# Keeping the emitted order on every engine, and emitting the softmax three superblocks ahead, late in the pass

## The chip, the cores and the metric

The kernel runs on one core of one Trainium2 chip. The time is device time in microseconds (us) of that core; a kernel's time is the median of its timed runs. The profile and trace are of one execution; its span (first to last instruction) lies about 2 us below the time.

Engines: PE is TensorE (PEld its weight loads), DVE is VectorE, ACT is ScalarE, POOL is GpSimd, SP is SyncE, which issues the loads and stores of this kernel (SPq in the profile).

## The reference

A dynamic convolution over time, then a feed-forward block. Cut to what matters:

```python
w = exp(weight_gen - max);  w = w / sum(w)              # softmax over K = 7 taps, per head
x_pad = zeros for K-1 steps, then x                     # each batch starts with zeros
y[b, s, h, g] = sum_k w[b, s, h, k] * x_pad[b, s + k, h, g]
h = y @ w_in                                            # 192 -> 2048
out = (h - tanh(h)) @ w_out                             # 2048 -> 192
```

There are 8 batches of 4096 steps and 32,768 tokens. The kernel works in 32 superblocks of 1024 tokens, 4 to a batch.

## The kernel before

Six stages work on different superblocks at once: load, softmax (exp on ScalarE; sum, reciprocal, multiply on VectorE, giving `wsm`), products (GpSimd, seven of them, giving `prod`), transposes with the sum over taps (`conv`: TensorE into PSUM, ScalarE copies to `convT`), first matmul with h - tanh(h) (`gemm1`: TensorE `ph`, ScalarE `th`, VectorE `gt`), second matmul (`gemm2`: TensorE `po`, ScalarE `out_sb`, store). Where `manual_schedule` doesn't hold an engine, a scheduler in the build may reorder that engine's instructions.

```python
    # every pool below has bufs=2: wgpool (wg_t, e_t, zsum, zr, wsm), xpool, ppool (prod0..6), opool (out_sb)
    # psum_h bufs=3 (ph and pc share it), psum_o bufs=2

    def load(n):                       # wg_t: 128 partitions
        ...
        lo = 0
        if s == 0:                     # first superblock of a batch: partition 0 has no history
            lo = 1
            nc.vector.memzero(x_t[0:1, 0:HALO, :])
            nc.sync.dma_start(out=x_t[0:1, HALO : HALO + J, :], in_=x[b, 0:J]...)
        ...
        nc.sync.dma_start(out=x_t[lo:P, :, :], in_=src)     # 127 partitions if s == 0

    def softmax(n):
        nc.scalar.activation(out=e_t, in_=wg_t, func=ACT.Exp)
        nc.vector.reduce_sum(out=zsum, in_=e_t)
        nc.vector.reciprocal(zr, zsum)
        nc.vector.tensor_mul(wsm, e_t, zr)

    def products(n):                   # 7 instructions on GpSimd
        for k in range(K):
            nc.gpsimd.tensor_mul(prod[k], x_t[:, k : k + J, :], wsm[:, :, :, k : k + 1])
    ...
    order = tc.manual_schedule(engines={mybir.EngineType.PE})
    ctx.enter_context(order)           # TensorE keeps the emitted order, the scheduler orders the rest
    ...
    for n in range(NTOT + 1):          # "pass n"
        if n + 2 < NTOT:
            softmax(n + 2)
            products(n + 2)
        if n + 3 < NTOT:
            load(n + 3)
        for p in range(J):             # J = 8
            gemm1(n, 2 * p); gemm1(n, 2 * p + 1)
            gemm2((n - 1) * J + p)
            if p == 2: conv(n + 1, (0, 1))
            if p == 5: conv(n + 1, (2,))
```

The softmax here doesn't subtract the row's maximum and nothing guards it: scores larger than these inputs give would overflow.

## Time and profile before

| | before |
|---|---|
| time, median | 1441.03 us (1439.78 to 1442.24) |
| span of the profiled run | 1437.9 us |
| busiest engine | TensorE, 58% |
| ordinary superblock | 40.9 us |
| four superblocks (a batch) | 174.1 us |

The page's first part gives busy time, share of the span and number of instructions of each engine; the groups give source line, engine, operation, shapes and count, then busy time and mean duration in ns, then the engine's idle time just before them and what ended most of it:

```profile
PE 837.2 (58%) x16640; PEld 639.2 (44%) x16640; DVE 662.3 (46%) x616; ACT 643.0 (45%) x865; POOL 654.4 (46%) x247
...
L124 POOL TENSOR_TENSOR prod<-x_t,wsm 128x1536 bf16<-128x1536 f32 x224 | 643.1, 2908 | 685.1 <-PE pc L147 613.3
L110 DVE TENSOR_TENSOR wsm<-e_t,zr 128x448 f32<-128x448 f32 x32 | 25.3, 792 | 352.1 <-POOL prod L124 352.1
```

No engine is near its limit. GpSimd is idle for 685 us, of which 613 end with TensorE's transposes; VectorE is idle for 352 us in front of 32 small multiplies, 23 times until GpSimd's products end. Each waits for the other.

### The profile page before, as it was taken

To read this page: it belongs to the slowest core of one execution; us is meant where nothing else is said; L and a number is where in the kernel's file an instruction comes from. 1 tells how busy PE (TensorE), PEld (TensorE's weight loads), DVE (VectorE), ACT (ScalarE), POOL (GpSimd) and SP (SyncE) were. 2 spreads that over 40 slices of the span, in tenths; PEclk is the share of its full clock that TensorE was granted. 3 is DMA by queue.
4 is the path that set the end of the run, shared out by engine and by line. 5 is a ranking of instruction groups with operands and counts; after the bars stand their busy time and mean duration, and the time that the engine had idled before them with its cause. 6 is when DMAs were issued, how large, how long until landed. Compare 5 with 4: busy or idle time off the path is not lost.

```text
span 1437.9 us, 36105 instructions
## 1 busy us (share of the span) xinstructions
PE 837.2 (58%) x16640; PEld 639.2 (44%) x16640; DVE 662.3 (46%) x616; ACT 643.0 (45%) x865; POOL 654.4 (46%) x247
## 2 busy tenths in 40 slices
PE   0033526774556755556755556655557753568997
PEld 0012425553444544444544445544345542456776
DVE  0034524553444544444544444544435553447783
ACT  0022424552444544444544444544335543456884
POOL 3098455433555315555145553445544435544700
PEclk9996868886888878888788888888878887788999
DMA  4321211112110121101211020110301102012011
GB/s 68 88 69 50 75 38 43 68 49 87 67 40 31 54 82 69 68 5 55 79 68 68 9 94 35 69 69 13 115 9 69 68 17 103 20 45 85 25 46 46
DMA packets 16951, 81.18 MB, mean 56 GB/s; under 512 B 4128, under 2 KB 8224, under 8 KB 12712
## 3 DMA queue, kind: packets, MB, share of 16 engines
q1 hardware_dynamic: 13712, 76.51, 14.1%
q0 software_dynamic: 3088, 2.36, 1.3%
q8 instruction: 130, 2.13, 0.6%
q14 instruction: 21, 0.17, 0.0%
HBM read 56.06 MB, written 25.17 MB: 56 GB/s over the span
## 4 chain that ended last, share of the span: by engine, by line
PE 38%; POOL 30%; DMA 14%; DVE 6%; another core or an unknown queue 5%; issue 5%; ACT 1%; POOLq 0%; DVEq 0%; ACTq 0%
POOL prod L124 30%; PE po L200 18%; PE ph L170 15%; DMA out_dram<-out_sb 12%; PE pc L147 5%; DVE gt L181 4%; DMA w_in<-in_moe_w_in_dram 2%; DVE wsm L110 1%; ACT th L179 1%; DVE x_t L83 0%; ACT out_sb L225 0%; DVE zsum L104 0%; ACT e_t L98 0%; POOLq L124 0%
## 5 line engine op out<-in xcount | busy, mean ns | idle before, releaser
L124 POOL TENSOR_TENSOR prod<-x_t,wsm 128x1536 bf16<-128x1536 f32 x224 | 643.1, 2908 | 685.1 <-PE pc L147 613.3
L181 DVE TENSOR_TENSOR gt<-ph,th 128x1024 bf16<-128x1024 f32 x512 | 601.5, 1215 | 219.2 <-ACT th L179 217.7
L170 PE MATMUL ph<-convT,w_in 64*128 64x512 bf16 x3072 | 416.5, 392 | 443.3 <-DVE gt L181 437.7
L179 ACT ACTIVATE th<-ph 128x1024 f32<-128x1024 f32 x512 | 501.2, 1021 | 94.2 <-PE ph L170 90.7
L200 PE MATMUL po<-w_out,gt 64*128 64x192 bf16 x8192 | 419.5, 255 | 48.9 <-ACT out_sb L225 47.9
L200 PEld LDWEIGHTS <-gt 64*128 64x128 bf16 x8192 | 388.1, 100 | 111.7 <-issue 64.1
L170 PEld LDWEIGHTS <-w_in 64*128 64x128 bf16 x3072 | 165.4, 96 | 576.3 <-issue 485.7
L98 ACT ACTIVATE e_t<-wg_t 128x448 f32<-128x448 f32 x32 | 18.4, 576 | 515.1 <-DVE wsm L110 437.9
L110 DVE TENSOR_TENSOR wsm<-e_t,zr 128x448 f32<-128x448 f32 x32 | 25.3, 792 | 352.1 <-POOL prod L124 352.1
L147 PE MATMUL pc<-ident,prod 64*128 64x64 bf16 x5376 | 101.8, 198 | 104.0 <-POOL prod L124 91.5
L147 PEld LDWEIGHTS <-prod 64*128 64x128 bf16 x5376 | 98.5, 100 | 105.9 <-POOL prod L124 92.4
L225 ACT ACTIVATE out_sb<-po 128x192 f32<-128x192 f32 x256 | 85.0, 332 | 117.0 <-PE po L200 64.7
L157 ACT ACTIVATE convT<-pc 128x1024 bf16<-128x1024 f32 x64 | 51.7, 810 | 63.6 <-PE pc L147 63.6
L83 DVE MEMSET x_t<- 1x1152 uint32 x8 | 8.1, 1018 | 104.3 <-POOL prod L124 103.2
L104 DVE TENSOR_REDUCE zsum<-e_t 128x64 f32<-128x448 f32 x32 | 19.5, 611 | 79.2 <-ACT e_t L98 79.2
L239 POOL DMA_DIRECT2D w_in<-in_moe_w_in_dram x16 | 9.4, 592 | 19.6 <-DMA w_in<-in_moe_w_in_dram 19.2
L108 DVE RECIPROCAL zr<-zsum 128x64 f32<-128x64 f32 x32 | 17.5, 547 | 0.5
L244 POOL DMA_DIRECT2D w_out<-in_moe_w_out_dram x1 | 1.2, 1206 | 1.9 <-DMA w_in<-in_moe_w_in_dram 1.9
L98 ACT ACT_TABLE_LOAD x1 | 1.3, 1283 | 0.7 <-PEq L289 0.7
masks.py:199 POOL TENSOR_SCALAR_AFFINE_SELECT ident<-ident 128x128 bf16<-128x128 bf16 x1 | 0.3, 304 | 0.1
masks.py:197 POOL MEMSET ident<- 128x128 bf16 x1 | 0.2, 205 | 0.3 <-POOLq L289 0.3
L289 POOL MEMSET const-float32-0.0<- 128x1 f32 x1 | 0.1, 98 | 0.2 <-issue 0.2
(3 smaller groups left out, 0.3 us busy)
## 6 DMA issues: line engine op xcount, KB each, us to landing
x_t<-in_x_dram SPq DMA_DIRECT2D x24, 1344.0 KB
out_dram<-out_sb SPq DMA_DIRECT2D x32, 768.0 KB
x_t<-in_x_dram SPq DMA_DIRECT2D x8, 1333.5 KB
wg_t<-in_weight_gen_dram SPq DMA_DIRECT2D x32, 224.0 KB
w_in<-in_moe_w_in_dram POOLq DMA_DIRECT2D x16, 96.0 KB, 18.8
w_out<-in_moe_w_out_dram POOLq DMA_DIRECT2D x1, 768.0 KB, 49.7
x_t<-in_x_dram SPq DMA_DIRECT2D x8, 6.0 KB
```

What stands on the lines that cost most here:

```text
L98: nc.scalar.activation(out=e_t[:].rearrange("p j h k -> p (j h k)"), in_=wg_t[:].rearrange("p j h k -> p (j h k)"), func=ACT.Exp,)
L104: nc.vector.reduce_sum(out=zsum[:], in_=e_t[:].rearrange("p j h k -> p (j h) k"), axis=AX.X)
L108: nc.vector.reciprocal(zr[:], zsum[:])
L110: nc.vector.tensor_mul(wsm[:].rearrange("p j h k -> p (j h) k"), e_t[:].rearrange("p j h k -> p (j h) k"), zr[:].rearrange("p (n o) -> p n ...
L124: nc.gpsimd.tensor_mul(prod[:].rearrange("p c j h g -> p j h c g"), x_t[:, k : k + J, :].rearrange("p j (h c g) -> p j h c g", h=H, c=NC), ...
L147: nc.tensor.matmul(pc[:, r, col : col + R], lhsT=prods[k][r * R : (r + 1) * R, c, 2 * j : 2 * j + 2].rearrange("p j h g -> p (j h g)"), rh ...
L157: nc.scalar.activation(out=convT[:, c0 : c0 + nch, :].rearrange("p c (j r t) -> p r (c j) t", r=2, t=R), in_=pc[:, :, 0 : nch * JH * R].re ...
L170: nc.tensor.matmul(ph[:, r, :], lhsT=w_in[r * R : (r + 1) * R, c, f * P : (f + 1) * P], rhs=convT[r * R : (r + 1) * R, c, :], start=(c == ...
L179: last_act[0] = nc.scalar.activation(out=th[:], in_=ph_f, func=ACT.Tanh)
L181: nc.vector.tensor_sub(gt[:], ph_f, th[:])
L200: mm = nc.tensor.matmul(po[:, 0:D], lhsT=g_of[n][f][r * R : (r + 1) * R, col : col + P], rhs=w_out[r * R : (r + 1) * R, f, :], start=(r == ...
L225: last_act[0] = nc.scalar.activation(out=out_sb[:, j, :], in_=po[:, 0:D], func=ACT.Copy)
```

## The change

The intent is to take the scheduler's freedom away from all engines, not only from TensorE, and to write the softmax where its inputs are ready and nothing waits for it yet.

```diff
-    order = tc.manual_schedule(engines={mybir.EngineType.PE})
-    ctx.enter_context(order)
+    ctx.enter_context(tc.manual_schedule())
...
     products(1)
+    softmax(2)
     for n in range(NTOT + 1):
         if n + 2 < NTOT:
-            softmax(n + 2)
             products(n + 2)
...
                 if p == 5:
                     conv(n + 1, (2,))
+            if p == 5 and n + 3 < NTOT:
+                softmax(n + 3)
```

## The prediction

> **What bounds the kernel now.** I read the chain of waits' totals first, then the timeline of one superblock, then windows of the last 130 us, then the SyncE queue. In the fences, T is the start of the 56-matmul transpose (third chunk, p = 5) of a pass; n counts passes of the loop; 4 superblocks make a batch.
>
> ```profile
> POOL prod L124 <- PE pc L147: 613.3, 28, 30.6
> PE ph L170 <- DVE gt L181: 437.7, 41, 25.8
> DVE wsm L110 <- POOL prod L124: 352.1, 23, 26.0
> ACT out_sb L225 <- DMA out_dram<-out_sb: 49.6, 6, 8.5
> ...
> 600.50 0.63 DVE L110 TENSOR_TENSOR wsm<-e_t,zr 128x448 f32<-128x448 f32 x1 [15.38 <-POOL prod L124]
> 602.32 1.46 PE L170 MATMUL ph<-convT,w_in 64*128 64x512 bf16 x6 [15.17 <-DVE gt L181]
> 621.03 1.00 PE L147 MATMUL pc<-ident,prod 64*128 64x64 bf16 x56
> 621.41 20.06 POOL L124 TENSOR_TENSOR prod<-x_t,wsm 128x1536 bf16<-128x1536 f32 x7 [20.94 <-PE pc L147]
> ```
>
> The first three totals form a ring. The scheduler put the wsm multiply of a later superblock into VectorE's stream so early that its buffer (two of them) is still read by GpSimd's products. VectorE stands 15.38 us at it with ready gt subtractions behind it, so the ph banks stay full, TensorE stands 15.17 us, and the transpose that frees the prod buffers comes 20 us later; only then does GpSimd start again (it idled 20.94 us). Products (20.06 us) and TensorE's pass (20.9 us) thus alternate: 41 us a superblock. No engine is over 58% busy, and that is no comfort: the engines take turns.
>
> The same kernel shows what it does without that ring, because after 1303 us no wsm is left to compute:
>
> ```profile
> 1316.59:1340.41 23.82, 23.73 (x526) 18.57 (x522) 18.85 (x17) 19.56 (x27) 20.07 (x7) 1.00 0.09 36
> 1364.23:1388.04 23.81, 23.71 (x526) 18.52 (x522) 18.84 (x16) 19.55 (x27) 0.00 (x0) 1.00 0.09 36
> ```
>
> Columns: stretch, length, busy TensorE, weight loads, VectorE, ScalarE, GpSimd, TensorE clock, DMA share, GB/s. A pass takes 23.82 us at full clock with TensorE busy for 23.73, and costs the same with the products running beside it as without.
>
> The fourth total has another source: the loads of x.
>
> ```profile
> 676.00:679.00 3.00, 0.00 (x0) 0.00 (x0) 0.00 (x0) 0.00 (x0) 3.00 (x2) 0.50 0.07 29
> ...
> 1163.60 0.24 SPq L84 DMA_DIRECT2D x_t<-in_x_dram  x1
> 1170.31 16.79 SPq L229 DMA_DIRECT2D out_dram<-out_sb  x1
> ...
> 351.80 2.74 PE po L200 x32
> 354.55 2.67 PE pc L147 x112
> ```
>
> The first superblock of a batch loads 127 partitions instead of 128. Such a load, issued at 641.79, still moves 25 to 29 GB/s at a DMA share of 0.07 (one engine in 16) past 690; its 127 packets last 0.404 us each, 51.3 us in all. Stores queued behind it land with it: of the one issued at 1170.31, the chain shows the end at 1220.7, which is 57.1 us after the load's issue at 1163.60. An ordinary x load runs at 355 GB/s (602 to 606), 4 us. The last two lines are TensorE just after such a store landed, cold.
>
> **What the Trainium skill says.**
> - PSUM — Partial Sum Buffer, section Engine vs sequencer instructions: the queues of ScalarE, VectorE and GpSimd are strict FIFO. The trace agrees: 15.38 us at wsm with gt work waiting.
> - DMA: Bandwidth & Descriptors, section on why a DMA increments its semaphore by 16: 127 partitions put everything on one DMA engine. The trace agrees (share 0.07, 26 GB/s).
> - SBUF — State Buffer, section Who interferes with whom: a VectorE instruction with two SBUF inputs contends with a GpSimd instruction that reads SBUF; with one, it doesn't. The trace agrees: wsm, started while products ran (95.09, 115.50), took 3.31 us instead of 0.62; gt, with one input in PSUM, doesn't lengthen in the windows above.
> - TensorE: Matmul & The Clock Gate, part 1: half clock after idling. Windows show 0.50 after idle stretches and 1.00 some 4 us into work.
>
> **The change, part by part.** It removes and adds no instruction; the built kernels have the same 618 VectorE rows, and 238 GpSimd rows in the same order. It moves 32 exps and their zsum, zr and wsm.
>
> *1. The ring opens.* softmax(n+3) now stands after conv(n+1) at p = 5. Its wsm buffer was last read by products(n+1), which start about T(n-2)+4.2 and end 20.06 us later, T(n-2)+24.3: before T(n-1), a whole pass ahead. So VectorE finds nothing to wait for, and products(n+3) run beside the next pass, needed only at p = 2 of pass n+2. A pass falls from 41 to the tail's 23.82 us plus what softmax adds. ScalarE has 19.56+0.58 = 20.1 us, VectorE 18.85+0.62+0.55+0.62 = 20.6, GpSimd 20.1: TensorE bounds.
>
> *2. What softmax adds at p = 5.* In the tail, relative to T = 1341.10, the convT copy ends at 1.64, th starts at 1.69, gt starts at 2.74, and frees the bank that the fourth following gemm1 takes at 4.33, with 0.3 us to spare. With exp first (pitch 0.49), zsum (0.66 pitch), zr (0.59) and wsm (0.55) on VectorE, gt starts at 1.69+0.61+0.66+0.59+0.55 = 4.10 instead of 2.74: 1.36 late, less 0.3 of slack, TensorE waits 1.05. VectorE then catches up (2.36 of work in 2.62 us per p). Pass: **24.87 us**.
>
> *3. The slow load.* x(n+3) takes the buffer of x(n+1), free at the end of products(n+1), so a slow load goes out at t0 = T(n-1)-0.5, behind it in the queue the store of superblock n-2, landing at t0+57.1 = T(n-1)+56.6. ScalarE needs that store's out_sb buffer at p = 1 of pass n+1: 24.87+12.8 = T(n-1)+37.7. ScalarE stands **18.9 us**, and TensorE with it, because both po banks wait for that copy. TensorE has run 0.7 ahead but resumes cold: 2.74+2.67 us in the lines above against about 3.06 warm, so +2.35. Another +0.7 for a wsm that meets the late products. Four passes: 4 x 24.87 + 18.9 - 0.7 + 2.35 + 0.7 = **120.7 us** per batch against 174.1 now (351.80 to 525.88). The late products, t0+54.5 to t0+75, are in time for their transpose at about t0+86, so that delay is hidden by the other.
>
> *4. Start and end.* x(0) is a slow load too and the change doesn't touch it: products(0) start at 74.6 again, products(1) end at 115.5, and three wsm in the first passes meet busy products (2 to 2.9 us each). Walking on: T(1) = 150, T(2) = 176.5. Pass 2 waits 14 us for weights behind slow load x(4), cold restart 2, products(4) 2 more, so T(3) = 220, T(4) = 247. The next load goes out 3.5 us late, T(8) = 371. Five batches of 120.7: T(28) = 974. Then 24.87 + 23.82 and the unchanged end (1388.74 to 1437.9, 49.2) give 1072. Seven x_t memsets on VectorE at a pass start, estimated at 0.4 us each, make the span 1075; the time lies 2 to 4 us above the span (1440.06 and 1442.06 against 1437.9): **1078 us**, 0.75 of the time now.
>
> **The rivals.**
> - *The slow loads are hidden.* If stores didn't wait for the one slow engine, only steps 1 and 2 would count: 1078 less 7 times about 20, 935 us. For it: the load itself has over a pass of lead. Against: 49.6 us of ScalarE waiting for out_dram in the trace now, six times, at 41 us a pass; a shorter pass leaves the load less cover.
> - *A new wait takes the ring's place.* wsm or exp could block at the new place, behind late products or late weights, and the engines take turns again, 1300 to 1440 us. The order of the built kernel speaks against it: the buffers are free a pass earlier. Only around slow loads could it last, as a second stall; at 10 us more each, 1150 us.
> - *The given order is poor.* ScalarE and VectorE lose the scheduler's interleaving; if the softmax bubble were 3 us, not 1, or the clock fell under longer work, passes of 26 to 27 us would make 1120 to 1140. The tail keeps clock 1.00 through 72 us of unbroken work and its order is already that of the code, which speaks against it.
>
> **Range and chances.** An error of 5 us in the stall moves the total by 35 us, one of 0.6 us in the pass by 18. I take 1040 to 1120. Even the worst rival but one is over 10% faster, so faster by over 2% has 0.97, within 2% 0.02, slower 0.01.
>
> **What would show it.** Step 1: the total of wsm waiting for prod falls from 352 to under 20 us, GpSimd idles about 4 us per pass, TensorE's share rises to about 75%. Step 2: T to T in an ordinary pass 24.9, with a wait of ph for gt near 1 us after each softmax. Step 3: ScalarE's out_sb waits for out_dram, six times, near 19 us each; a batch every 121 us. Step 4: products(0) at 74.6. The prediction is wrong if wsm still waits for GpSimd in each pass, or out_sb doesn't wait for the store.

## The result, and the profile after

| | before | after |
|---|---|---|
| time, median | 1441.03 us | 1084.88 us (1083.28 to 1087.66) |
| ratio | | 0.7531 (95% interval 0.7513 to 0.7548) |
| mean TensorE clock granted | 0.835 | 0.924 |
| ordinary superblock | 40.9 us | 24.74 us |
| batch | 174.1 us | 122.2 us |

A ratio is the mean time of one kernel's fast runs over the mean of the other's in the same rounds, so it is not quite the ratio of the medians quoted. The batch after is the mean of five, from the first load at 252.43 us to the one at 863.64.

The same lines of the page, after:

```profile
PE 801.6 (74%) x16640; PEld 614.9 (57%) x16640; DVE 676.3 (62%) x616; ACT 642.6 (59%) x865; POOL 655.0 (60%) x247
...
L124 POOL TENSOR_TENSOR prod<-x_t,wsm 128x1536 bf16<-128x1536 f32 x224 | 643.7, 2910 | 332.3 <-DMA x_t<-in_x_dram 267.6
L110 DVE TENSOR_TENSOR wsm<-e_t,zr 128x448 f32<-128x448 f32 x32 | 34.4, 1076 | 2.7
```

The work is the same, TensorE's share rose from 58 to 74%, and VectorE's wait before wsm is gone: 2.7 us instead of 352.1. GpSimd no longer waits for transposes but for loads of x. The totals of waits (who waited for whom: us in total, times, longest):

```profile
POOL prod L124 <- DMA x_t<-in_x_dram: 267.6, 8, 41.2
ACT out_sb L225 <- DMA out_dram<-out_sb: 120.6, 6, 23.5
PE po L200 <- ACT out_sb L225: 118.9, 15, 22.6
PE ph L170 <- DVE gt L181: 51.0, 41, 11.6
```

TensorE's wait for gt fell from 437.7 to 51.0 us. Its wait for out_sb, behind a store, rose from 47.9 to 118.9. The chain that ended last gives 30% of the span before to GpSimd's products, and 1% after; stores went from 12 to 22%. So the time went where the ring was, and what is left over is the slow load.

Two ordinary passes after, as windows (length; busy PE, PEld, DVE, ACT, POOL; clock, DMA share, GB/s), and the softmax in one of them in the timeline:

```profile
353.74:378.48 24.74, 23.90 (x524) 18.47 (x520) 20.46 (x20) 20.00 (x27) 20.06 (x8) 1.00 0.15 50
...
352.92 0.62 DVE L110 TENSOR_TENSOR wsm<-e_t,zr 128x448 f32<-128x448 f32 x1
353.68 20.07 POOL L124 TENSOR_TENSOR prod<-x_t,wsm 128x1536 bf16<-128x1536 f32 x7 [4.67 <-PE po L200]
354.73 0.82 PE L170 MATMUL ph<-convT,w_in 64*128 64x512 bf16 x6 [0.75 <-DVE gt L181]
```

A pass has TensorE busy for 23.90 of 24.74 us, at full clock. After the softmax it waits 0.75 us. And this is the slow part of the same batch (start, us, then the instruction, and in brackets its engine's idle time before it and what ended that):

```profile
373.77 0.24 SPq L84 DMA_DIRECT2D x_t<-in_x_dram  x1
384.62 11.77 SPq L229 DMA_DIRECT2D out_dram<-out_sb  x1
429.27 20.06 POOL L124 TENSOR_TENSOR prod<-x_t,wsm 128x1536 bf16<-128x1536 f32 x7 [30.80 <-DMA x_t<-in_x_dram]
431.07 0.33 ACT L225 ACTIVATE out_sb<-po 128x192 f32<-128x192 f32 x1 [19.11 <-DMA out_dram<-out_sb]
431.45 2.74 PE L200 MATMUL po<-w_out,gt 64*128 64x192 bf16 x32 [18.20 <-ACT out_sb L225]
447.20 2.62 DVE L110 TENSOR_TENSOR wsm<-e_t,zr 128x448 f32<-128x448 f32 x1
451.01 1.24 PE L170 MATMUL ph<-convT,w_in 64*128 64x512 bf16 x6 [2.74 <-DVE gt L181]
```

The load of 127 partitions is issued at 373.77 (with its small companion for partition 0), the store behind it at 384.62. The x arrives 55.5 us after its issue, the store 57.2 us after the load's issue (the chain gives 46.36 us from the store's issue to its end). ScalarE stands 19.11 us, TensorE 18.20. Then the late products are still running when the next wsm comes at 447.20; it takes 2.62 us instead of 0.62, and TensorE waits a second time.

### The profile page after: what moved, and what is told of

It reads as the page before. It is cut to its first block, busy times and chain, and to the rows that moved or that the text cites. A ratio compares the mean times of both kernels' runs of the same rounds, so it can differ in the third digit from the quotient of the medians.

```text
span 1082.9 us, 36083 instructions
## 1 busy us (share of the span) xinstructions
PE 801.6 (74%) x16640; PEld 614.9 (57%) x16640; DVE 676.3 (62%) x616; ACT 642.6 (59%) x865; POOL 655.0 (60%) x247
## 4 chain that ended last, share of the span: by engine, by line
PE 47%; DMA 22%; DVE 10%; another core or an unknown queue 3%; issue 2%; ACT 2%; POOL 1%; DVEq 0%; ACTq 0%
PE po L200 22%; DMA out_dram<-out_sb 22%; PE ph L170 19%; PE pc L147 6%; DVE gt L181 5%; DVE wsm L110 3%; DVE zsum L104 1%; POOL prod L124 1%; ACT e_t L98 1%; DVE zr L108 1%; ACT out_sb L225 0%; ACT th L179 0%; ACT convT L157 0%; DVEq L110 0%
## 5 line engine op out<-in xcount | busy, mean ns | idle before, releaser
L200 PE MATMUL po<-w_out,gt 64*128 64x192 bf16 x8192 | 398.5, 247 | 119.9 <-ACT out_sb L225 118.9
L200 PEld LDWEIGHTS <-gt 64*128 64x128 bf16 x8192 | 366.0, 96 | 175.5 <-issue 124.1
L170 PE MATMUL ph<-convT,w_in 64*128 64x512 bf16 x3072 | 404.6, 383 | 55.0 <-DVE gt L181 51.0
L147 PE MATMUL pc<-ident,prod 64*128 64x64 bf16 x5376 | 99.5, 195 | 101.8 <-POOL prod L124 100.4
L147 PEld LDWEIGHTS <-prod 64*128 64x128 bf16 x5376 | 95.1, 98 | 104.7 <-POOL prod L124 102.0
L98 ACT ACTIVATE e_t<-wg_t 128x448 f32<-128x448 f32 x32 | 18.2, 568 | 83.2 <-DMA wg_t<-in_weight_gen_dram 83.2
L110 DVE TENSOR_TENSOR wsm<-e_t,zr 128x448 f32<-128x448 f32 x32 | 34.4, 1076 | 2.7
```

The source lines that it names most:

```text
L98: nc.scalar.activation(out=e_t[:].rearrange("p j h k -> p (j h k)"), in_=wg_t[:].rearrange("p j h k -> p (j h k)"), func=ACT.Exp,)
L110: nc.vector.tensor_mul(wsm[:].rearrange("p j h k -> p (j h) k"), e_t[:].rearrange("p j h k -> p (j h) k"), zr[:].rearrange("p (n o) -> p n ...
L147: nc.tensor.matmul(pc[:, r, col : col + R], lhsT=prods[k][r * R : (r + 1) * R, c, 2 * j : 2 * j + 2].rearrange("p j h g -> p (j h g)"), rh ...
L170: nc.tensor.matmul(ph[:, r, :], lhsT=w_in[r * R : (r + 1) * R, c, f * P : (f + 1) * P], rhs=convT[r * R : (r + 1) * R, c, :], start=(c == ...
L200: mm = nc.tensor.matmul(po[:, 0:D], lhsT=g_of[n][f][r * R : (r + 1) * R, col : col + P], rhs=w_out[r * R : (r + 1) * R, f, :], start=(r == ...
```

## The experiments

Theory A: the scheduler wrote wsm so far ahead in VectorE's stream that it waits for products that have only just begun; the gain is that ring gone, and what is left is the 127-partition load. Theory B: the late place in the code is what opens the ring. Theory C: the kept order helps in some other way (ScalarE, the queues). All results were correct; each ratio is against the kernel before on the same chip.

| run | what differs | us | ratio to before (95%) |
|---|---|---|---|
| e1_order_only | before + kept order | 1107.80 | 0.7688 (0.7675 to 0.7700) |
| e2_place_only | before + late place | 1441.44 | 1.0008 (0.9991 to 1.0025) |
| e8_early_by_hand | kept order, softmax(n+4) early | 1322.91 | 0.9179 (0.9165 to 0.9193) |
| e9_early_three_wsm | e8 + third wsm buffer | 1128.22 | 0.7825 (0.7812 to 0.7838) |
| e3_split_load | after + load as 112 and 15 | 881.89 | 0.6118 (0.6104 to 0.6133) |
| e4_before_split_load | before + load as 112 and 15 | 1325.54 | 0.9195 (0.9181 to 0.9209) |
| e5_three_out | after + third out_sb buffer | 1053.17 | 0.7315 (0.7299 to 0.7332) |
| e10_split_softmax | e3 + softmax in two parts | 857.26 | 0.5947 (0.5938 to 0.5956) |
| e11_order_split | e1 + load as 112 and 15 | 902.25 | 0.6264 (0.6255 to 0.6272) |
| e12_place_split | e3 again | 882.32 | 0.6115 (0.6098 to 0.6131) |

### The two halves of the change

`e1_order_only` takes only this from the change:

```diff
-    order = tc.manual_schedule(engines={mybir.EngineType.PE})
-    ctx.enter_context(order)
+    ctx.enter_context(tc.manual_schedule())
```

> The first half of the change alone: every engine keeps the emitted order, but softmax(n+2) stays at the head of the pass. Theory A (the ring was made by the scheduler, which pulled wsm two superblocks further ahead than the code writes it): the ring opens here too, because wsm(n+2) at the head of pass n waits for products(n), which are long done; ordinary passes of 24.7 us. Each slow load then goes out about 6 us later against the pass (products start at the head, not at p = 5), so ScalarE stands some 25 to 27 us at out_sb instead of 20: about 1135 us. Theory B (the late place is what opens the ring): wsm goes on waiting for products in each pass, 1400 to 1440 us.

It took 1107.80 us. The ring is open: VectorE has no wait of wsm for products in its list, and ordinary products start 25.5 us apart. The forecast of 1135 was too slow: ScalarE's waits at out_sb came to 134.9 us for six, 22.5 each, not 25 to 27, while the passes were longer than the 24.7 us forecast, which hides part of that error.

`e2_place_only` takes the other half: softmax(2) ahead of the loop and softmax(n+3) after conv at p = 5, with the old schedule line.

> The second half alone: softmax(n+3) is emitted late, but only TensorE keeps the emitted order and the scheduler places the rest. Theory A: the scheduler pulls the softmax ahead again, wsm waits some 350 us for products in all, about 1440 us, within 2% of the kernel before. Theory B: the late place opens the ring, about 1085 us.

```profile
POOL prod L124 <- PE pc L147: 613.2, 28, 30.6
DVE wsm L110 <- POOL prod L124: 352.3, 23, 26.6
```

It took 1441.44 us, and these totals are those of the kernel before (613.3 and 352.1). The scheduler undid the late place altogether. So theory B falls: of the 356 us that the change gained, the kept order alone gives 334 (1441.56 - 1107.80), the place alone nothing, and the place on top of the kept order 23 (1107.80 - 1084.88, from two sets of rounds).

### The ring made and opened by hand

Is it the scheduler as such, or where it put wsm? In the trace of before, the wsm that VectorE meets in pass 2, at 212.05, is the seventh of the run (superblock 6), four ahead of the pass. `e8_early_by_hand` keeps every engine's emitted order and emits just that. The load is split so that weights come early enough, and ahead of the loop (not in the cut) one superblock more is loaded and put through softmax.

```diff
         if n + 2 < NTOT:
             products(n + 2)
+        if n + 4 < NTOT:
+            softmax(n + 4)
         if n + 3 < NTOT:
-            load(n + 3)
+            load_x(n + 3)
+        if n + 5 < NTOT:
+            load_w(n + 5)
...
-            if p == 5 and n + 3 < NTOT:
-                softmax(n + 3)
```

> Every engine keeps the emitted order, but the code itself now emits softmax(n+4) at the head of pass n, where the scheduler had put it in the kernel before (weights loaded a pass earlier for it). Theory A (the ring is a matter of where wsm stands in VectorE's stream): the ring comes back without any scheduler, VectorE waits some 12 to 15 us for products in nearly every pass, passes of 41 us, 1400 to 1450 us. Theory C (the scheduler did other harm, in ScalarE's or the queues' order, and the gain comes from the kept order as such): about 1085 to 1110 us.

```profile
POOL prod L131 <- PE pc L154: 397.3, 22, 21.1
PE ph L177 <- DVE gt L188: 387.9, 35, 36.6
DVE wsm L117 <- POOL prod L131: 337.0, 29, 16.0
```

The ring is back, with nothing scheduled: wsm waits for products 29 times, 11.6 us each, and products start 39 us apart (307.99 to 464.09 for four). The time, 1322.91 us, is below the range that theory A gave. The ring is 2 us shorter a pass than in the kernel before; and ScalarE never waits for a store. The store was issued at 317.09, 27.5 us after the slow load at 289.56, so it should land near 347, an estimate from the 57.2 us above; the next store of the stream goes out at 357.39, and only after that is the buffer wanted. So no cost of the slow load is seen: products start 37.9 to 40.4 us apart across it. Theory C falls: the kept order with a bad place has the ring again.

`e9_early_three_wsm` is the same code with a pool of its own for wsm:

```diff
+    wsmpool = ctx.enter_context(tc.tile_pool(name="wsmpool", bufs=3))
...
-        wsm = wgpool.tile([P, J, H, K], FP32, name="wsm")
+        wsm = wsmpool.tile([P, J, H, K], FP32, name="wsm")
```

> The same early order with three wsm buffers instead of two, nothing else. Theory A: wsm(n+4) then takes the buffer that products(n+1) have long left, the ring is open, and the time is that of the kept order, some 1100 to 1140 us; it can be a little over e1_order_only because wsm now meets running products in each pass (up to 2.9 us). Theory C, or a ring through another buffer: no better than with two, 1400 us or more.

One buffer more took 195 us off: 1128.22. wsm waits for products only once. But it now starts while products run, in three passes of four:

```profile
508.56 3.22 DVE L118 TENSOR_TENSOR wsm<-e_t,zr 128x448 f32<-128x448 f32 x1
...
512.97 1.46 PE L178 MATMUL ph<-convT,w_in 64*128 64x512 bf16 x6 [3.85 <-DVE gt L189]
516.77 2.52 PE L178 MATMUL ph<-convT,w_in 64*128 64x512 bf16 x12
```

The multiply takes 3.22 us instead of 0.62, TensorE waits 3.85 us, and goes on cold (2.52 us for 12 matmuls, which take 1.47 warm). Products start 30.7 us apart (499.82 to 530.53). So the hand-made pair shows the ring to be a matter of place and buffers, and shows besides what the late place of the change avoids in ordinary passes: at p = 5 the products have ended.

### The slow load

`e3_split_load` changes only how the first superblock of a batch is loaded:

```diff
-        nc.sync.dma_start(out=x_t[lo:P, :, :], in_=src)
+        for p0, p1 in ((0, P),) if lo == 0 else ((1, P - 15), (P - 15, P)):
+            ...                       # same source pattern, from partition p0
+            nc.sync.dma_start(out=x_t[p0:p1, :, :], in_=src)
```

> The changed kernel, with the 127 partitions at a batch's start loaded as 112 and 15. If the slow load is the whole cause of ScalarE's wait for the store, that wait (120.6 us) and GpSimd's for x (267.6 us) go to near zero, each batch takes 4 x 24.74 = 99 us instead of 122.5 (seven of them: -164 us), and products(0) start at about 34 us, when the weight loads have been issued, instead of 74.6 (-41 us): about 880 us. If the wait has another cause (the store itself, or full queues), it stays above 1030 us.

It took 881.89 us, 203 less than the changed kernel, and the forecast was 880. No wait of ScalarE for a store is left in the list. The first products of the run start at 26.86 us, not 74.64, so some 48 of the 203 us are gained at the start; a batch takes 99.3 us (loads at 480.43 and 579.76). The same edit without the change, `e4_before_split_load`:

> The kernel before with the 127-partition load split into 112 and 15, the ring left in. If the two causes add up independently, a batch falls from 174.1 us to four ordinary passes of 40.9 (-10.5 us, seven times: -73) and the start falls by the 48 us that it fell in e3_split_load: about 1320 us, 0.916 of before. If the slow load had a share in the ring, much less: under 1250 us.

It took 1325.54 us. The ring is untouched (wsm waits 337.4 us), and the products still start 40.8 us apart:

```profile
340.18 20.06 POOL L125 TENSOR_TENSOR prod<-x_t,wsm 128x1536 bf16<-128x1536 f32 x7 [20.63 <-PE pc L148]
381.00 20.06 POOL L125 TENSOR_TENSOR prod<-x_t,wsm 128x1536 bf16<-128x1536 f32 x7 [20.76 <-PE pc L148]
```

So the two causes are separate, but they don't add up: the split load is worth 116 us in the kernel before and 203 in the changed one. Some 45 to 48 us of each lie at the start (first products at 29.4 and 26.86 us); the rest is per batch, where a shorter pass leaves a 55-us load less to hide behind.

### What lay hidden behind the store

The prediction said that the late products lie behind ScalarE's wait for the store. `e5_three_out` takes the store's wait away and leaves the slow load:

```diff
-    opool = ctx.enter_context(tc.tile_pool(name="opool", bufs=2))
+    opool = ctx.enter_context(tc.tile_pool(name="opool", bufs=3))
```

> The changed kernel with three out_sb buffers instead of two, the slow load untouched. Then the store that is stuck behind it is needed a pass later, some 6 us after it lands, and that wait goes. The prediction held that the late products were hidden behind the store's wait; without it they should come out: products(n+3) end 75 us after the load's issue and their transpose would come at about 65, so TensorE waits some 10 us for products, and ScalarE's exp up to 6 us for weights within that. About 10 us of each stall are saved, some 1015 to 1025 us. If the store alone limits, 930 us; if late products or weights cost as much as the store, 1085 us.

It took 1053.17 us. The wait for the store went, as all theories had it, but only 32 us were gained, not 60 to 70:

```profile
ACT e_t L98 <- DMA wg_t<-in_weight_gen_dram: 136.6, 9, 71.9
...
544.48 0.58 ACT L98 ACTIVATE e_t<-wg_t 128x448 f32<-128x448 f32 x1 [8.63 <-DMA wg_t<-in_weight_gen_dram]
546.40 2.06 DVE L110 TENSOR_TENSOR wsm<-e_t,zr 128x448 f32<-128x448 f32 x1
549.65 1.47 PE L170 MATMUL ph<-convT,w_in 64*128 64x512 bf16 x6 [10.93 <-DVE gt L181]
561.23 1.90 PE L147 MATMUL pc<-ident,prod 64*128 64x64 bf16 x112
```

What came out was first of all the weights, stuck in the same queue: exp waits 8.63 us for them, then meets late products (wsm 2.06 us), and TensorE waits 10.93 us. The next wsm meets products again (3.01 us). At 589.54 the chain has a stop of 2.34 us inside the transposes and calls it issue; that products caused it is not shown, since those that these transposes read had ended at about 582.7. But the late products are not cleared: they run from 542.22 to 562.28, and the transposes that read them from 561.23 to 563.13. Had the weights not held TensorE for 10.93 us, it would have stood some 10 us for the products instead (an estimate from these times). So the prediction was right that another wait lay behind the store's. The weights' wait comes first, and the products' wait lies behind it in turn.

### The place of the softmax

How much is the late place worth where no slow load disturbs? `e11_order_split` is `e1_order_only` with the split load, and `e12_place_split` repeats `e3_split_load` on the same chip; they differ by the place alone.

> The kept order with softmax(n+2) at the head of the pass and the split load: the place alone against e12_place_split, without slow loads. In e1_order_only TensorE waited 1.08 us for gt after each softmax at the head against 0.75 at p = 5; if that is all the place is worth in a pass, 29 passes make 10 us: about 892 us, and the other 13 us between e1_order_only and the changed kernel came from the longer waits at the slow loads (134.9 against 120.6 us of ScalarE). If the whole 0.78 us that the passes of e1_order_only were longer by belongs to the place, 905 us. If the place is worth nothing but through slow loads, 882.

> e3_split_load once more, on the same chip as e11_order_split, to be compared with it: 882 us again, passes of 24.74 us.

They took 902.25 and 882.32 us: the place is worth 20 us, between the 10 of the first forecast and the 23 of the second. At the head of the pass TensorE waits 1.25 us after each softmax, not 0.75:

```profile
483.44 0.82 PE L171 MATMUL ph<-convT,w_in 64*128 64x512 bf16 x6 [1.25 <-DVE gt L182]
```

Ordinary products start 25.25 us apart (457.13 to 482.38) against 24.74. Some 29 passes of 0.5 us are 15 us. The rest lies in the passes of a batch's first load. At the head, four of six start 26.4 us apart and two 28.05 and 27.90, against 25.2 at p = 5. One of each kind, as windows:

```profile
404.08:431.98 27.90, 25.40 (x520) 19.43 (x520) 21.64 (x21) 20.04 (x28) 20.06 (x8) 0.94 0.31 99
507.62:534.03 26.41, 23.90 (x520) 18.45 (x520) 21.55 (x21) 20.05 (x28) 20.06 (x8) 1.00 0.32 104
```

In all six TensorE waits 2.39 us at the head, where softmax and the memset of x_t (1.02 us) stand close together in VectorE's stream; in the two longer ones it then ran at the low clock for a while. Beyond the 0.5 us counted already, the six come to some 7 us, so 22 with the 15 (an estimate; 20 were measured). That the memset is what adds up there was not tried by itself.

`e10_split_softmax` asks whether the last 0.75 us is the softmax: exp, zsum and zr go before the transposes at p = 2, wsm before those at p = 5, into gaps that ScalarE and VectorE have there.

```diff
+            if p == 2 and n + 3 < NTOT:
+                softmax(n + 3)        # exp, zsum, zr only
+            if p == 5 and n + 3 < NTOT:
+                scale(n + 3)          # wsm
             if n + 1 < NTOT:
                 if p == 2:
                     conv(n + 1, (0, 1))
...
-            if p == 5 and n + 3 < NTOT:
-                softmax(n + 3)
```

> The changed kernel with the split load and with softmax cut in two: exp, zsum and zr before the first transpose at p = 2, where ScalarE idles 1.3 us and VectorE 2.2 us, and wsm before the second at p = 5, where VectorE idles 1.1 us and GpSimd has finished its products. If the 0.92 us that an ordinary pass has over 23.82 us is the softmax bubble at p = 5, it goes: 29 passes, -26 us against e3_split_load's 882, about 855 us. If it is something else that comes with busy neighbours, the time stays at 882.

```profile
PE 772.6 (90%) x16640; PEld 598.2 (70%) x16640; DVE 678.1 (79%) x616; ACT 643.7 (75%) x865; POOL 653.6 (76%) x247
...
159.96 20.06 POOL L130 TENSOR_TENSOR prod<-x_t,wsm 128x1536 bf16<-128x1536 f32 x7 [3.75 <-PE ph L176]
183.78 20.06 POOL L130 TENSOR_TENSOR prod<-x_t,wsm 128x1536 bf16<-128x1536 f32 x7 [3.76 <-PE ph L176]
```

It took 857.26 us, 25 less than `e3_split_load` (they ran on different chips, against the same kernel before), with 26 forecast. Products start 23.82 us apart, exactly the pass of the tail of the kernel before, which had no softmax at all. TensorE is busy for 90% of the span. This version beats both kernels: 0.5947 of before.

## Why the prediction was right, and by how much its terms were off

The time was forecast at 1078 us, with 1040 to 1120 as the range, and measured at 1084.88.

**Step 1, the ring, was right.** wsm's wait for products left the list, GpSimd idles 4.68 us in an ordinary pass, TensorE's share is 74% (75 forecast). That the place in the stream and the buffer count make the ring was argued then and is shown now, by the pair made by hand. What the prediction did not ask is which half of the change does it; it told the mechanism by the late place, and the kept order would have been enough to open the ring.

**Step 2, the softmax bubble, was right in kind.** It was forecast at 1.05 us, a pass of 24.87; measured 0.75 of waiting and a pass of 24.74, 0.92 over the tail's 23.82. `e10_split_softmax` shows that all of it is the softmax.

**Step 3, the slow load, was right in its cause and in its largest term, and two smaller terms were off.** Store landing 57.2 us after the load's issue (57.1 forecast), ScalarE's wait 19.11 and TensorE's 18.20 in the batch shown (18.9 and 18.2 forecast), on average 20.1 us for the six. Cold restart: from 431.45 to the next gemm1 at 435.72 is 4.27 us against 2.95 warm in the pass before (363.22 to 366.17), so 1.3, not 2.35. The wsm that meets late products was the undersized term: forecast 0.7, but TensorE waits 2.74 us there, 2.0 more than in an ordinary pass, and falls back to the low clock once more. From 451.01 to the gemm1 at 454.56 are 3.55 us against 1.96 in an ordinary pass (354.73 to 356.69), 1.6 more. Taken together, 1.9 us more a batch (2.0 + 1.6 - 0.7 - 1.0), and 0.5 less from the four shorter passes, which makes 122.1 instead of 120.7; the batch shown took 122.88 (373.77 to 496.65), the five 122.2 on average. It was luck that the restart, put too high, cancelled a third of what the wsm was put too low.

**The claim that the late products are hidden by the store's wait** was right as far as it went, and incomplete: `e5_three_out` showed that the weights, late in the same queue, stop TensorE before the products can.

**Step 4, start and end.** Products(0) start at 74.64 (74.6). T(28), the last transpose of the third chunk with a softmax behind it, was forecast at 974 and stands at 985.14: 2.4 us come from the first slow load after the start (252.43 instead of 250), some 8 from five batches of 1.5 us. From there to the end are 97.8 us, as forecast (24.87 + 23.82 + 49.2). The memsets, counted extra with 3 us, are within the batches.

Left open: in the profile of `e1_order_only` the ordinary windows have a clock of 0.95 where the other kept-order kernels with two wsm buffers have 1.00, though that kernel's other runs, with a higher mean clock (0.92 instead of 0.89), took the same time. So how its 23 us over the changed kernel divide between the place and the slow loads was not taken from it, but from `e11_order_split`.

## What to carry to other kernels

When no engine is over 60% busy and two of them wait for each other in the totals of waits, look for an instruction that stands in an in-order stream ahead of work that is ready, and ask which buffer it waits for: one more buffer, or a later place, may be worth more than any faster instruction. After such a change the next bound is often something that was hidden by the slack: here a load that had cost some 10 us a batch came to cost over 20, and fixing it was worth 203 us instead of 116 (some 45 to 48 of each at the start). Put small work of a shared engine into gaps that the timeline shows, one instruction at a time if need be.

## What the Trainium skill lacked or had wrong

- **TensorE: Matmul & The Clock Gate, part 1** gives the low clock after an idle window of about 3.4 us. Here a pause of 2.74 us (448.27 to 451.01 in the changed kernel) was enough; the windows of one us from 450 show it:

```profile
450.00:451.00 1.00, 0.00 (x0) 0.00 (x0) 1.00 (x2) 0.00 (x0) 1.00 (x1) 1.00 0.60 129
451.00:452.00 1.00, 0.99 (x6) 0.42 (x7) 1.00 (x1) 0.00 (x0) 1.00 (x1) 0.64 1.08 366
452.00:453.00 1.00, 1.00 (x15) 1.00 (x13) 1.00 (x2) 0.72 (x1) 1.00 (x2) 0.50 1.02 387
```

  The length alone did not decide: in `e11_order_split` TensorE paused 2.39 us at the head of six passes, and went on at the low clock after two of them (the window from 404.08, shown above, clock 0.94) and at full clock after four (1.00).

- **DMA: Bandwidth & Descriptors**, where it says that 127 partitions put everything on one engine, gives no figure for what that costs the transfers behind it in the same queue. Here a store of 128 partitions landed only 57.2 us after the slow load's issue, and SyncE was held while it issued the next transfer: 11.77 us for the store at 384.62, and 20.40 and 22.16 us for weight loads issued behind two other slow loads. I found no page that gives a duration for this hold.
